# A filter moved into columns by transposes against a permutation, with the sign taken over by VectorE

## The chip, the cores and the metric

The kernel runs on one core of one Trainium2 chip. The metric is the device time of one execution in microseconds (us). All times below are us from the first instruction of the profiled execution unless they are marked ns. The engines are called as the profile calls them: PE is the matrix engine (PEld its weight loads), DVE is VectorE, ACT is ScalarE, POOL is GpSimd, SP is SyncE, whose queue issues most of the DMAs.

## The reference

A global filter in the frequency domain, followed by a mixture of experts in which each expert keeps at most 80 tokens:

```python
# x: (8, 2496, 256); filt_r, filt_i: (1249, 256), that is 2496 // 2 + 1 frequencies by 256 channels
X = np.fft.rfft(x, axis=1)
Y = X * (filt_r + 1j * filt_i)[None, :, :]
y = np.fft.irfft(Y, n=2496, axis=1)          # then reshaped to (19968, 256)

logits = y @ w_gate                          # w_gate: (256, 8)
expert_idx = np.argmax(logits, axis=1)       # gate_w: the softmax value of that expert
for e in range(8):                           # tokens of expert e, the 80 with the largest gate_w
    h = np.maximum(y[tok_idx] @ w1[e], 0.0)  # w1[e]: (256, 1024)
    out[tok_idx] = gate_w[tok_idx, None] * (h @ w2[e])
# all other rows of out are zero
```

## The kernel before

The transform of length 2496 is done as 39 by 64. The work has a first phase over "half batches" h (16 of them: 8 batches of 2 channel blocks of 128) and a second phase that picks tokens, rebuilds only the picked rows and runs the experts. The order of the instructions on every engine is written out by hand and kept; the framework only adds the semaphores. So a line further down in the program never overtakes a line above it on the same engine.

The first phase has 80 steps k, five for each half batch h. One step of the loop (from L969) writes, in this order:

- for k from 0 to 8 a filter turn (`next_filter`, L972; described below);
- `turn_t(k+1)` (L320): four PE transposes `pt` of 128x128 against the identity, then an ACT copy `t`;
- `stage2(k)` (L331): four matmuls `pb` against the table `d_t`;
- `filtered(k)` (L340): DVE multiplies the PSUM result by the filter `ft` into `p` (L346), and POOL adds and subtracts the halves into `yt` (L354, two instructions);
- from k = 4 on, one or two pieces of `stage1` of a later half batch (L304): matmuls `pa` against `wf_t` and an ACT copy `tt`;
- from k = 2 on `turn_y(k-2)` (L362): a DVE block transpose `u` of `yt`, whose result goes to DRAM (`yf`).

The filter arrives in rows and is needed in columns. `fst` is one tile of 128 partitions, 20 slots s and 256 channels. Partitions 0 to 63 hold the real part and 64 to 127 the imaginary part; in each half the lower 32 partitions are frequencies read upwards and the upper 32 are frequencies read downwards, so that those stand for the mirrored (conjugated) half of the spectrum. Partitions 96 to 127 are the mirrored imaginary rows. `filter_in(g)` (L497) issues four DMAs for a group g of four slots, two on SP's queue (real) and two on POOL's (imaginary), all five groups ahead of the loop. `filter_turn(g, cb)` (L506) multiplies the four slots of one channel block by a table `perm` of 0, 1 and -1, which orders the rows by frequency, and copies the result from PSUM to `ft`. There are ten turns: the first five are channel block 0 of g = 0 to 4, the last five are channel block 1. The first is written ahead of the loop with its copy on DVE (L910), the other nine stand at the top of the steps k = 0 to 8 with their copies on ACT, one step ahead of the `filtered` that needs them. Step k holds turn number k + 1.

The PSUM pool of these results has six buffers. `x` comes in three pieces for each batch through SP's queue; the pieces 3 to 6 are issued behind all of the real filter's DMAs, and the first `stage1` of the loop (step 4) reads the first of them.

Of the kernel before, what the change touches and what calls it, by code (L numbers as in the profile page):

```python
# [10 lines left out]
AL = mybir.AluOpType  # L11
# [19 lines left out]
SG, NG = 4, 5  # L31
# [15 lines left out]
def dft_tables():  # L47
    n1, n2 = np.arange(N1), np.arange(N2)
    s, q = np.arange(NS), np.arange(NQ)
    ph = 2 * np.pi * (np.outer(n1, s) % N1) / N1  # L50
    w = np.stack([np.cos(ph), -np.sin(ph)], 2)
    wf = np.zeros((N1, H3, NS, 2, H3))
    for h in range(H3):
        wf[:, h, :, :, h] = w

    slot = [J3 * h + j for j in range(20) for h in range(3)]
    slot += [J3 * h + j for j in range(20, J3) for h in range(2)]
    k = np.array([[next(m for m in range(i, S, N1) if m % NQ == j) for j in q] for i in s])
    th = 2 * np.pi * (n2[slot][:, None, None] * k % S) / S
    c, sn = np.cos(th), np.sin(th)  # L60
    d = np.zeros((2, N2, NS, 2, NQ))
    d[0, :, :, 0], d[1, :, :, 0] = c, sn
    d[0, :, :, 1], d[1, :, :, 1] = -sn, c

    two = np.where(s == 0, 1.0, 2.0) / S
    be = 2 * np.pi * (np.outer(q, n2) % NQ) / NQ
    back = np.zeros((2, NQ, 2, N2))
    back[0, :, 0], back[1, :, 0] = np.cos(be), -np.sin(be)
    back[0, :, 1], back[1, :, 1] = np.sin(be), np.cos(be)
    wi = np.zeros((4, SP, 2, N1, 4))  # L70
    for e in range(4):
        wi[e, :NS, 0, :, e] = (two * np.cos(ph)).T
        wi[e, :NS, 1, :, e] = (-two * np.sin(ph)).T

    n = (39 * n2[:, None] + 64 * n1) % S
    al = 2 * np.pi * (n.reshape(S, 1, 1) * k % S) / S
    rows = np.stack([np.cos(al), -np.sin(al)], 2) * two[:, None, None]
    at = np.arange(128)
    rows = rows.reshape(S, NS, 128)[:, :, 32 * (at % 4) + at // 4]
    rows = rows.reshape(S, NS, 4, 32).transpose(0, 2, 1, 3)  # L80

    perm = np.zeros((2, 2, 32, 2, NQ + NS - 1))
    for i in range(32):
        for up, t in enumerate((2 * 32 - 1 - i, i)):
            for j in range(NQ + NS - 1):
                if (j - 39 * t - NS + 1) % NQ == 0:
                    perm[0, 1 - up, i, 0, j] = 1.0
                    perm[1, 1 - up, i, 1, j] = 1.0 if up else -1.0
    f32 = np.float32
    return (wf.reshape(NP1, NM1).astype(f32), wi.reshape(4 * SP, 2, 4 * N1).astype(f32),  # L90
            d.reshape(128, NS, 128).astype(f32), back.reshape(128, 128).astype(f32),
            rows.reshape(S, NS * 128).astype(f32),
            perm.reshape(128, 2 * (NQ + NS - 1)).astype(f32))
# [3 lines left out]
def kernel(  # L97
# [11 lines left out]
    nc = tc.nc  # L109
    assert 1 <= cap <= 128  # L110
    cap1 = -(-cap * CAP1 // 80)

    wf_host, wi_host, d_host, e_host, rows_host, perm_host = dft_tables()
    wf_dram = nc.inline_tensor(wf_host, name="wf_tbl")
    wi_dram = nc.inline_tensor(wi_host, name="wi_tbl")
# [28 lines left out]
    def part_of(name, op, by, add=0.0):  # L144
# [26 lines left out]
                            op0=AL.mult, op1=AL.add)  # L171
    for b in range(B):
        nc.vector.tensor_scalar(out=cbase[:, b, :], in0=iota[:, 0:KC], scalar1=float(PB),
                                scalar2=4096.0 * b + 1.0, op0=AL.mult, op1=AL.add)
    nc.vector.tensor_scalar(out=cbase[:], in0=cbase[:], scalar1=trow[:, 0:1], scalar2=None,
                            op0=AL.add)
# [3 lines left out]
                            op0=AL.is_equal)  # L180
    thot = const([128, 16], F32, "thot")
    nc.vector.tensor_scalar(out=thot[:], in0=iota[:, 0:16], scalar1=trow[:, 0:1], scalar2=None,
                            op0=AL.is_equal)
    same_f = const([128, 128], F32, "same_f")
    with tc.tile_pool(name="setup", bufs=1) as su:
# [6 lines left out]
                                op0=AL.is_equal)  # L192
# [4 lines left out]
                            op0=AL.is_gt)  # L197
# [10 lines left out]
                            op0=AL.add)  # L208
# [45 lines left out]
    with tc.manual_schedule():  # L254
# [19 lines left out]
        perm = fwd.tile([128, 2, NQ + NS - 1], F32, name="perm")  # L274
        fst = late.tile([128, NS, C], F32, name="fst", tag="page0")
# [228 lines left out]
                                    ap=[[N1 * C, 32], [step, SG], [1, C]]))  # L504

        def filter_turn(g, cb, copy):  # L506
            ps = fps.tile([128, SG, 2, NQ], F32, name=f"pf_{g}_{cb}", tag="f")
            for i in range(SG):
                s = SG * g + i
                nc.tensor.matmul(out=ps[:, i], lhsT=fst[:, s, 128 * cb:128 * cb + 128],  # L510
                                 rhs=perm[:, :, NS - 1 - s:NS - 1 - s + NQ],
                                 start=True, stop=True)
            copy(out=ft[:, :, cb, SG * g:SG * g + SG, :].rearrange("p v s q -> p s v q"),
                 in_=ps[:])

# [298 lines left out]
        for i in range(5):  # L814
            nc.vector.tensor_scalar(out=shifted[:, i, :], in0=iota[:, 0:KR],
                                    scalar1=1.0 - (8 >> i), scalar2=None, op0=AL.add)
# [80 lines left out]
        def next_filter(copy):  # L897
            if turns:
                filter_turn(*turns.pop(0), copy)
# [69 lines left out]
        for k in range(NK):  # L969
# [8 lines left out]
            for h, i in s1_steps(k):  # L978
                stage1(h, i)
                hb, cb = divmod(h, NDB)  # L980
# [147 lines left out]
        for e in range(NH):  # L1128
            nc.gpsimd.indirect_dma_start(
                out=xg[e][:], out_offset=None, in_=y_sel[0:128 * (NR - 1), :],  # L1130
# [600 lines left out]
```

## Time and profile before

| what | value |
|---|---|
| runs | 407.19, 409.98 and 409.0 us (median 409.0) |
| the profiled execution, its own time | 407.02 us |
| its span, first to last instruction | 405.2 us |
| PE busy | 356.4 us, 88% of the span |
| DVE busy | 236.1 us, 58% |
| ACT busy | 132.8 us, 33% |
| POOL busy | 181.1 us, 45% |
| mean granted PE clock | 0.971 |

The profile has several views. The page gives the busy time of each engine, the chain of work that ended last (followed back from the last instruction, at each step to what released it) and the costliest groups of instructions: line, engine, operation, output <- inputs, count, then busy time and mean ns of one, then idle time ahead of them. The timeline merges neighbouring instructions of one line into a row: start, duration, engine, line, operation, names, shapes, count, and in brackets the engine's idle time ahead of the row and what ended it. PE records an ordinary float32 matmul as two passes, so a count of 8 can be four instructions (the ten filter turns are 40 matmuls and 80 records). The table by stretches gives for each stretch of time the busy time of each engine, the granted PE clock and the share of the DMA engines.

### The profile page before, as it was taken

How to read it: one execution, taken by the hardware profiler on the slowest of the kernel's cores; microseconds unless marked ns; L12 is line 12 of the kernel's file. 1: busy time of each engine (PE TensorE's matmuls, PEld its weight loads, DVE VectorE, ACT ScalarE, POOL GpSimd, SP SyncE). 2: the span in 40 equal slices, each digit the busy share in tenths (PEclk: the TensorE clock that was granted, in tenths of full speed). 3: DMA queues.
4: the chain of work that ended last, by engine and by line, in shares of the span. 5: the costliest groups of instructions: out<-in, count | busy, mean ns of one | idle time of the engine just before them, and what ended most of it. 6: DMA issues, size and time to landing. Idle time of an engine off the chain costs nothing.

```text
span 405.2 us, 9718 instructions
## 1 busy us (share of the span) xinstructions
PE 356.4 (88%) x3973; PEld 318.8 (79%) x3973; DVE 236.1 (58%) x485; ACT 132.8 (33%) x274; POOL 181.1 (45%) x248
## 2 busy tenths in 40 slices
PE   2879999999999999899999998979999857967970
PEld 2879979989989899699799896857875527957950
DVE  5025557766977858879798898299777400201100
ACT  1434545445445455354454452240100000101010
POOL 8335444644655545555457767730661010221220
PEclk9999999999999999999999999999999995989896
DMA  7998799999989989978999998999999995496000
GB/s 219 236 216 257 183 320 252 275 332 250 315 268 258 333 248 254 328 203 286 309 245 272 364 271 269 405 402 392 410 406 389 385 372 181 147 313 227 26 23 10
DMA packets 41099, 109.92 MB, mean 271 GB/s; under 512 B 4202, under 2 KB 14312, under 8 KB 39176
## 3 DMA queue, kind: packets, MB, share of 16 engines
q1 hardware_dynamic: 36534, 95.94, 74.0%
q0 software_dynamic: 4240, 13.15, 9.3%
q8 instruction: 33, 0.54, 0.5%
q10 hardware_dynamic: 274, 0.14, 0.1%
q14 instruction: 18, 0.15, 0.1%
HBM read 70.42 MB, written 40.37 MB: 273 GB/s over the span
## 4 chain that ended last, share of the span: by engine, by line
PE 49%; DMA 32%; issue 8%; POOL 3%; DVE 3%; ACT 2%; SPq 1%; POOLq 0%; ACTq 0%; DVEq 0%
PE pa L311 15%; PE pb L336 15%; PE pt L325 8%; DMA y_sel<-yr 7%; DMA x<-in_x_dram 6%; DMA out_dram<-ys_True,idxs 6%; DMA gt<-rows_tbl,idxr 4%; PE pz L390 4%; DMA page<-yf 3%; DMA xg_True<-y_sel,idxg 3%; PE pr L867 2%; DMA fst<-in_filt_r_dram 2%; ACT tt L316 1%; POOL gt L844 1%; PE py L402 1%
## 5 line engine op out<-in xcount | busy, mean ns | idle before, releaser
L354 POOL TENSOR_TENSOR yt<-p 128x256 f32<-128x256 f32 x156 | 113.5, 749 | 104.2 <-DVE p L346 95.5
L346 DVE TENSOR_TENSOR p<-pb,ft 128x1024 f32<-128x1024 f32 x80 | 97.2, 1217 | 53.1 <-PE pb L336 24.5
L311 PE MATMUL pa<-wf_t,x 117*128 117x120 f32 x704 | 92.7, 279 | 8.9 <-DMA x<-in_x_dram 8.2
L311 PEld LDWEIGHTS pa<-wf_t,x 117*128 117x128 f32 x704 | 86.9, 196 | 9.1 <-issue 7.6
L336 PE MATMUL pb<-d_t,t 128*128 128x128 f32 x640 | 84.6, 275 | 1.5 <-ACT t L329 1.5
L336 PEld LDWEIGHTS pb<-d_t,t 128*128 128x128 f32 x640 | 77.7, 192 | 1.9 <-ACT t L329 1.9
L316 ACT COPY tt<-pa 128x480 f32<-128x480 f32 x96 | 47.9, 516 | 91.3 <-PE pa L311 90.2
L867 PE MATMUL pr<-page,wt 128*32 128x256 f32 (+1 forms) x520 | 63.8, 380 | 1.8 <-DVE wt L855 1.0
L867 PEld LDWEIGHTS pr<-page,wt 128*32 128x32 f32 (+1 forms) x520 | 45.5, 134 | 16.2 <-issue 1.8
L325 PE MATMUL pt<-ident,tt 128*128 128x128 f32 x320 | 49.4, 276 | 3.7 <-ACT tt L316 3.7
L329 ACT COPY t<-pt 128x512 f32<-128x512 f32 x80 | 47.1, 589 | 16.1 <-PE pt L325 15.1
L367 DVE STREAM_TRANSPOSE u<-yt 128x512 f32<-128x512 f32 x70 | 49.0, 700 | 0.0
L844 POOL DMA_INDIRECT gt<-rows_tbl,idxr x28 | 29.7, 1060 | 31.6 <-DVE idxr L686 13.2
L325 PEld LDWEIGHTS pt<-ident,tt 128*128 128x128 f32 x320 | 36.5, 141 | 7.5 <-ACT tt L316 4.6
L855 DVE STREAM_TRANSPOSE wt<-gt 128x640 f32<-128x640 f32 x28 | 22.5, 828 | 13.8 <-DMA gt<-rows_tbl,idxr 13.0
L1221 POOL DMA_INDIRECT out_dram<-ys_True,idxs x8 | 7.5, 932 | 34.3 <-ACT ys_True L1219 21.7
L872 ACT COPY yr<-pr 128x256 f32<-128x256 f32 x7 | 2.7, 379 | 57.7 <-DMA y_sel<-yr 33.0
L1179 PE MATMUL ph_True<-xs_True,w 128*64 128x80 f32 x512 | 20.6, 244 | 0.0
L1179 PEld LDWEIGHTS ph_True<-xs_True,w 128*64 128x64 f32 x512 | 19.9, 147 | 0.1
L1197 PE MATMUL po_True<-hT_True,w 128*64 128x80 f32 x448 | 19.8, 255 | 0.0
L1197 PEld LDWEIGHTS po_True<-hT_True,w 128*64 128x64 f32 x448 | 18.7, 155 | 0.8 <-issue 0.4
L390 PE MATMUL pz<-yt,wg 128*32 128x512 f32 (+1 forms) x256 | 18.9, 435 | 0.0
(217 smaller groups left out, 282.1 us busy)
## 6 DMA issues: line engine op xcount, KB each, us to landing
out_dram<-zero_t SPq DMA_DIRECT2D x32, 624.0 KB
yf<-u SPq DMA_DIRECT2D x56, 320.0 KB
w<-in_moe_w_dram SPq DMA_DIRECT2D x16, 1024.0 KB
page<-yf SPq DMA_DIRECT2D x24, 640.0 KB
x<-in_x_dram SPq DMA_DIRECT2D x16, 936.0 KB
x<-in_x_dram SPq DMA_DIRECT2D x7, 702.0 KB
page<-yf POOLq DMA_DIRECT2D x4, 640.0 KB, 8.9
fst<-in_filt_r_dram SPq DMA_DIRECT2D x10, 128.0 KB
```

The costliest lines, as they stand in the source:

```text
L311: nc.tensor.matmul(out=ps[:, j, :], rhs=wf_t, start=True, stop=True, lhsT=xt[3 * b + ch][:, j0 + j - JC * ch, 128 * cb:128 * cb + 128])
L316: nc.scalar.copy(out=tt[h][:, :, H3 * j0:H3 * j0 + hn * jn].rearrange("p s (j h) -> p s j h", h=hn), in_=v)
L325: nc.tensor.transpose(ps[:, i, :], tt[h][:, 2 * s:2 * s + 2, :].rearrange("p r n -> p (r n)"), ident[:])
L329: nc.scalar.copy(out=t2[k][:], in_=ps[:])
L336: nc.tensor.matmul(out=ps[:, :, i, :], lhsT=t[:, i, :], rhs=d_t[:, SG * g + i, :], start=True, stop=True)
L346: nc.vector.tensor_tensor(out=p[:], in1=f.unsqueeze(2).to_broadcast(shape), op=AL.mult, in0=ps[:].rearrange("p r s q -> p r (s q)").unsque ...
L354: eng.tensor_tensor(out=y[:, :, 2 * r:2 * r + 2, :], in0=a, in1=b, op=op)
L367: nc.vector.transpose(uu[h][:, :, SG * g:SG * g + SG, :].rearrange("p a s w -> p s a w"), spectrum(h)[:, SG * g:SG * g + SG])
L390: nc.tensor.matmul(out=ps[32 * j:32 * j + 32].rearrange("p (s w) -> p s w", s=pn), lhsT=wg[:, cb, :], rhs=yt_t[:, (2 * b + cb) % 2, 5 * j ...
L867: nc.tensor.matmul(st["po"][c:c + w, :], lhsT=wts[r][:, s, c:c + w], rhs=yt_t[:, :, s] if b == B - 1 else columns(pages[b], s), start=(s = ...
L1179: nc.tensor.matmul(ph[c:c + 64, i, 0:cap], lhsT=w1[:, k, f:f + 64], rhs=xs[:, k, :], start=(k == 0), stop=(k == NDB - 1))
L1197: nc.tensor.matmul(po[c:c + 64, d, 0:cap], lhsT=w2[:, fc, 128 * d + c:128 * d + c + 64], rhs=hT[:, fc, :], start=(fc == 0), stop=(fc == NF ...
```

## The change

The host table `perm` loses its minus sign and so holds only zeros and ones, a plain permutation. The filter turn's matmuls are issued as transposes, with that permutation where the identity usually stands. The sign is put back by DVE: ahead of the first turn of each group (channel block 0), it multiplies partitions 96 to 127 of the group's four slots by -1 in place, 32 partitions of 1024 float32. That makes five new DVE instructions; the turns of channel block 1 read the same rows, negated already.

```diff
             for j in range(NQ + NS - 1):
                 if (j - 39 * t - NS + 1) % NQ == 0:
                     perm[0, 1 - up, i, 0, j] = 1.0
-                    perm[1, 1 - up, i, 1, j] = 1.0 if up else -1.0
+                    perm[1, 1 - up, i, 1, j] = 1.0
...
         def filter_turn(g, cb, copy):
+            if cb == 0:
+                low = fst[96:128, SG * g:SG * g + SG, :]
+                nc.vector.tensor_scalar(out=low, in0=low, scalar1=-1.0, scalar2=None,
+                                        op0=AL.mult)
             ps = fps.tile([128, SG, 2, NQ], F32, name=f"pf_{g}_{cb}", tag="f")
             for i in range(SG):
                 s = SG * g + i
                 nc.tensor.matmul(out=ps[:, i], lhsT=fst[:, s, 128 * cb:128 * cb + 128],
                                  rhs=perm[:, :, NS - 1 - s:NS - 1 - s + NQ],
-                                 start=True, stop=True)
+                                 is_transpose=True, start=True, stop=True)
             copy(out=ft[:, :, cb, SG * g:SG * g + SG, :].rearrange("p v s q -> p s v q"),
                  in_=ps[:])
```

The instructions of DVE in the first steps then stand in this order: negation 0, copy of turn 0, negation 1, `p` of step 0, negation 2, `p` of step 1, negation 3, `p` of step 2, `u`, negation 4, `p` of step 3.

## The prediction

> **What bounds the kernel now.** I read the page first, for the span and the chain that ended last.
>
> ```profile
> span 405.2 us, 9718 instructions
> PE 49%; DMA 32%; issue 8%; POOL 3%; DVE 3%; ACT 2%; SPq 1%; POOLq 0%; ACTq 0%; DVEq 0%
> ```
>
> PE is half of that chain and DMA a third, so the question is what the chain runs through where the filter turns stand. The chain in order of time, cut to the first 52 us and to the seam of the two phases, says it:
>
> ```profile
> 2.79 15.17 DMA x<-in_x_dram
> 17.98 8.86 DMA fst<-in_filt_r_dram
> 26.85 10.67 DMA x<-in_x_dram
> 37.66 1.12 PE pa L311 x8
> 38.79 0.90 PE pf L510 x8
> 39.69 0.44 PE pt L325 x4
> 40.12 0.89 PE pb L336 x8
> ...
> 241.35 1.12 SPq L829
> 242.52 6.79 DMA page<-yf
> ```
>
> The columns are start, duration and what. Up to 37.66 the end is set by arriving data: x, the filter, x again. From 37.66 PE follows PE, step by step, up to the seam near 241. A turn that ends at 37 or before is hidden by the x transfer; a turn behind 37.66 stands on the path. PE's timeline places the turns (`pf`):
>
> ```profile
> 21.95 1.06 PE L510 MATMUL pf<-perm,fst 128*128 128x128 f32 x8
> 24.19 1.13 PE L510 MATMUL pf<-perm,fst 128*128 128x128 f32 x8 [1.18 <-DMA fst<-in_filt_r_dram]
> 25.60 1.06 PE L336 MATMUL pb<-d_t,t 128*128 128x128 f32 x8
> 26.97 1.13 PE L510 MATMUL pf<-perm,fst 128*128 128x128 f32 x8 [0.32 <-DMA fst<-in_filt_r_dram]
> 30.05 1.13 PE L510 MATMUL pf<-perm,fst 128*128 128x128 f32 x8 [0.62 <-DMA fst<-in_filt_r_dram]
> 32.44 1.13 PE L510 MATMUL pf<-perm,fst 128*128 128x128 f32 x8
> 34.73 1.06 PE L510 MATMUL pf<-perm,fst 128*128 128x128 f32 x8
> 37.66 1.12 PE L311 MATMUL pa<-wf_t,x 117*128 117x120 f32 x8 [0.54 <-DMA x<-in_x_dram]
> 50.20 1.50 PE L311 MATMUL pa<-wf_t,x 117*128 117x120 f32 x12
> ```
>
> Turns 0 to 5 start at 21.95 to 34.73, ahead of the x wait; turns 6 to 9 (steps 5 to 8) lie between 37.66 and 50.20. The x wait itself is only 0.54 us: anything that lengthens the steps before it by more than that moves the path.
>
> **The change part by part.** *What it removes.* A turn is four matmuls, and the page's transposes are the nearest row for their new form:
>
> ```profile
> L510 PE MATMUL pf<-perm,fst x80: 273/273/348, 21.9 to 48.8; 128*128 128x128 f32 x80
> L325 PE MATMUL pt<-ident,tt 128*128 128x128 f32 x320 | 49.4, 276 | 3.7 <-ACT tt L316 3.7
> ```
>
> Ten turns of four matmuls are 80 records, two passes each; 80 groups of four transposes are 320, one pass each. In the chain eight passes of a turn take 0.90 us and four of `pt` 0.44, so a turn gets 0.45 us shorter. All ten would give 4.5 us; the four behind 37.66 give 4 x 0.45 = 1.8 us on the path, and the six before it nothing, as long as the x wait covers them. That the rows of `perm` are not the identity should not alter the pass count; if it does, see the rivals.
>
> *What it adds.* Five DVE instructions of 32 x 1024 float32, and each of the first five turns now waits for one. No row shows this form. The nearest:
>
> ```profile
> L815 DVE TENSOR_SCALAR shifted<-iota 128x16 f32<-128x16 f32 x5 | 0.6, 163 | 0.0
> L187 DVE TENSOR_SCALAR m_i<-iota_i 128x128 int32<-128x128 int32 x1 | 0.2, 219 | 0.0
> L191 DVE TENSOR_SCALAR same_f<-m_f,lane 128x128 f32<-128x128 f32 x1 | 0.3, 278 | 0.0
> ```
>
> Constant operand: 163 ns at 16 elements, 219 at 128, so 0.5 ns an element and 219 + 896 x 0.5 = 667 ns at 1024. With a per-partition operand: 278 at 128, which against 163 is 1.03 ns an element and 278 + 896 x 1.03 = 1.2 us. The negation has a constant operand; I take 0.67 us, and 1.2 as the upper end.
>
> Its data do not hold it up. The imaginary rows come through POOL's queue:
>
> ```profile
> 4.47 4.54 POOL L501 DMA_DIRECT2D fst<-in_filt_i_dram  x8
> 13.94 0.55 POOL L501 DMA_DIRECT2D fst<-in_filt_i_dram  x1 [0.83 <-DMA fst<-in_filt_i_dram]
> DMA to landing us min/median/max: 7.9/8.6/11.6
> ```
>
> Groups 0 to 3 are issued by 9.0 and so landed by 20.6 at the longest, group 4 by 26.1. No DMA is moved, and SP's and POOL's queues are passed by nothing new.
>
> *Where the wait falls.* DVE executes in the written order, and negation g stands behind `p` of step g - 2:
>
> ```profile
> 23.05 0.69 DVE L513 COPY ft<-pf 128x512 f32<-128x512 f32 x1 [15.81 <-PE pf L510]
> 26.69 1.23 DVE L346 TENSOR_TENSOR p<-pb,ft 128x1024 f32<-128x1024 f32 x1 [2.95 <-PE pb L336]
> 33.85 0.70 DVE L367 STREAM_TRANSPOSE u<-yt 128x512 f32<-128x512 f32 x1
> ```
>
> So a ring closes that was open before: `p` (DVE), negation (DVE), next turn (PE), `pt`, `pb` (PE), `p` again. Before, PE ran ahead of DVE and the turn waited at most for its DMA. While PE waits at a turn, the transposes, `pb` and, from step 4, `pa` wait behind it, and ACT's copies behind those. The ring from rows: a hop between engines 0.04 (the copy at 23.05 starts 0.04 behind 21.95 + 1.06); turn to `pb` start 25.60 - 24.19 = 1.41, less 0.45, 0.97; `pb` start to `p` start 26.69 - 25.60 = 1.09; `p` 1.23; negation 0.67. One round is 4.00 us.
>
> - Negation 0 is done long before 21.95. Turn 0 ends 0.45 earlier, its copy is done at 23.30, negation 1 at 23.97: turn 1 still starts at 24.19, when its real rows arrive. No loss.
> - Turn 1 at 24.19, `pb` 25.16, `p` 26.25 to 27.48, negation 2 to 28.15, turn 2 at 28.19 (before: 26.97).
> - One round on: turn 3 at 32.19 (before: 30.05). Its data came at 30.05, so the ring decides.
> - `p` of step 2 ends at 35.48. Behind it now stands `u`, 0.70 with 0.08 overlapped: 36.10. Negation 4 to 36.77, turn 4 at 36.81 (before: 32.44).
> - Turn 5 needs no negation, the ring ends. `pb` of step 3 at 37.78, then eight passes (0.89), turn 5 and `pt` (0.45 each), `pb` of step 4 (0.89): the first `pa` at 40.45. The x wait is over by then and gone; what was late last, x, is replaced by the ring.
>
> That is 40.45 - 37.66 = 2.8 us late. Turns 6 to 9 give 1.8 back: **1.0 us late** at the row 50.20.
>
> *Contention.* POOL starts its two additions right behind `p`, and DVE and POOL can block each other:
>
> ```profile
> 28.00 1.41 POOL L354 TENSOR_TENSOR yt<-p 128x256 f32<-128x256 f32 x2 [5.29 <-DVE p L346]
> 113.38 0.14 DVE L467 TENSOR_SCALAR gw<-gw 128x39 f32<-128x39 f32 x1
> 161.83 1.41 POOL L354 TENSOR_TENSOR yt<-p 128x256 f32<-128x256 f32 x2 [1.20 <-DVE p L346]
> 162.69 0.59 DVE L467 TENSOR_SCALAR gw<-gw 128x39 f32<-128x39 f32 x1
> ```
>
> The same small constant-operand instruction takes 0.14 us at 113.38 and 0.59 at 162.69, ending at 163.28 where POOL's pair ends (163.24). The Trainium skill, page "SBUF — State Buffer", section "SBUF: two separate sides", calls it an exclusive lock held for a whole instruction by whichever of the two came first; by that rule, with which 162.69 agrees, a negation that comes second waits and one that comes first makes POOL wait. POOL starts 0.08 behind the end of `p` (28.00 against 27.92). Negations 2 and 3 are next on DVE and need no signal, so I let them win: cost nothing, `yt` some 0.6 later, which nothing in these steps waits for (`u` of it is two steps on). Negation 4 comes 0.62 behind the end of `p`, inside POOL's pair, which lasts to 0.08 + 1.41 = 1.49: it waits 0.17 (to the pair's middle, 0.79) to 0.87 us. I take 0.2, as one instruction ended the wait at 162.69.
>
> *Sum.* -1.8 + 2.8 + 0.2 = +1.2 us. From 50 to 241 the chain names engines alone and no DMA, and the loads at the seam are issued by those steps in order, so I carry it to the end one for one. The profiled execution took 407.02, which is 405.2 and 1.8 around it, and would take 408.2. The median of the runs shown is 409.0, which becomes **410.2 us**, 0.3% up.
>
> **The rivals.**
>
> *A. The ring is cheaper than drawn, faster.* If the negations left PE's order as it is (ring hidden whole behind the x transfer), only the 1.8 us would stay: 407.2. For it: DVE is idle between its rows there (2.95 ahead of 26.69). Against it: the queue's order, and an x slack of 0.54.
>
> *B. Dearer negations.* At 1.2 us each, negation 1 ends at 24.50 and delays turn 1 by 0.35, and three rounds grow by 0.53: +1.9 more, 412.1. If POOL wins the lock each time, negations 2 and 3 wait one or two instructions, 0.7 to 1.4 each, and negation 4 up to 0.7 more: 411.6 to 413.7. The first has against it that L191 has an operand of another kind; the second, POOL's start 0.08 behind.
>
> *C. The clock drops, slower.* PE would now idle from the end of `pb` to the next turn: 25.16 + 0.89 to 28.19 is 2.1 us, twice, and once 2.9. The tail shows what a gap can do:
>
> ```profile
> 367.59 2.44 PE L1197 MATMUL po_True<-hT_True,w 128*64 128x80 f32 x64
> 374.88 0.53 PE L1164 MATMUL px_True<-ident,xg_True 80*128 80x80 f32 x2 [2.29 <-DMA xg_True<-y_sel,idxg]
> 375.33 3.66 PE L1197 MATMUL po_True<-hT_True,w 128*64 128x80 f32 x64
> 265.00:266.20 1.20, 0.00 (x0) 0.00 (x0) 1.17 (x4) 1.20 (x4) 0.90 (x2) 1.00 1.04 410
> ```
>
> A gap of 2.29 was followed by 64 passes in 3.66 instead of 2.44; yet the stretch at 265 lies in a longer gap and its granted clock (third number from the end) is 1.00. One drop costs about 1.2: 411.4. If the clock halves and stays so for the three rounds, 16 passes of 0.11 double in each, 1.8 a round, 5.3 in all: 415.5. It is slower by over 1% (4.1 us) from the second such round on: 1.2 + 2 x 1.8 = 4.8. The Trainium skill, page "TensorE: Matmul & The Clock Gate", section "Part 4: PE-mode transpose", says that transposes do not count as activity to the clock gate; by that rule the new turns and `pt` would be idle time to it and only `pb` would hold the clock, which gives the long form, 415.5. No row of before shows such a mix with gaps of that length.
>
> *D. The permutation runs at two passes.* Nothing saved: four turns behind 37.66 and five in or behind the ring keep their 0.45, +4.0: 414.2. It would show as 80 records again.
>
> **How the numbers follow.** The forecast has 0.58, A 0.10, B 0.15, C 0.12 (two thirds of it the single drop), D 0.03, and 0.02 is for the order of the last DMAs falling otherwise. The runs of one kernel lie 2.8 us apart (407.19 to 409.98), so one per cent, 4.1 us, is about what tells a change from none. The forecast alone spans 409.4 to 411.5. The range takes in A and most of B and the single drop, with that scatter at the ends: 406.8 to 413.5. Faster by over 1% (below 404.9) lies under every case, 0.04. Slower by over 1% (above 413.1) takes C's long form, D and the top of B, 0.11. The rest, 0.85, is no change.
>
> **What would show it.** 40 `pf` records in place of 80, a turn of 0.45 us. Five DVE rows on `fst` of about 0.67 us, the last with a wait. PE waiting for DVE at turns 2, 3 and 4, 2.1 + 2.1 + 3.1 = 7.3 us in all. No wait for x ahead of the first `pa` of the loop, which starts at 40.5 to 40.8. Later steps moved by 1.0 to 1.4. Wrong if the negations run ahead of `p`, if the clock reads under 1.00 between 26 and 41, or if the seam or the tail gives back or adds more than the shift.

## The result, and the profile after

| | before | after |
|---|---|---|
| median of the runs | 408.25 us (405.13 to 412.43) | 413.11 us (410.14 to 417.15) |
| profiled execution, its own time | 407.02 | 415.02 |
| its span | 405.2 | 413.2 |
| its mean granted PE clock | 0.971 | 0.955 |

The ratio of after to before is 1.0135 [1.0109, 1.016]: slower by 1.35%, about 5.5 us, where 1.2 us was forecast. Carried to the median of 409.0 that the forecast started from, it gives 414.5, past the upper end of the range (413.5) and in the class to which 0.11 was given. The ratios here leave out executions in a slower state that some runs fall into, and are not the quotient of the two medians, which would be 1.0119.

From the page of the changed kernel: the span, the granted clock of PE in 40 slices (10.3 us each, tenths of full speed), and the chain by engine.

```profile
span 413.2 us, 9641 instructions
PEclk9986899999999999999999999989999997989995
PE 63%; DMA 13%; issue 10%; DVE 6%; ACT 3%; another core or an unknown queue 2%; POOL 1%; POOLq 0%; ACTq 0%; DVEq 0%
```

Before, DMA held 32% of the chain; now 13%, and PE 63%. Most of that difference lies behind the seam of the two phases: in the opening the chain held 34.7 us of transfers before and holds 23.2 now. The x transfer no longer sets the end of the opening. The new thing is in the clock: the third to fifth slices, 20.7 to 51.7 us, read 8, 6, 8. The timeline of PE on the changed kernel shows what lies there (start, duration, form, count, idle time ahead and what ended it):

```profile
24.08 0.93 PE L514 MATMUL pf<-perm,fst 128*128 128x128 f32 x4 [1.82 <-DMA fst<-in_filt_r_dram]
25.66 1.91 PE L336 MATMUL pb<-d_t,t 128*128 128x128 f32 x8
29.65 0.63 PE L514 MATMUL pf<-perm,fst 128*128 128x128 f32 x4 [2.08 <-issue]
30.56 1.06 PE L336 MATMUL pb<-d_t,t 128*128 128x128 f32 x8
33.77 0.63 PE L514 MATMUL pf<-perm,fst 128*128 128x128 f32 x4 [2.16 <-issue]
34.83 1.92 PE L336 MATMUL pb<-d_t,t 128*128 128x128 f32 x8
39.64 1.09 PE L514 MATMUL pf<-perm,fst 128*128 128x128 f32 x4 [2.89 <-issue]
41.37 1.92 PE L336 MATMUL pb<-d_t,t 128*128 128x128 f32 x8
45.66 1.05 PE L311 MATMUL pa<-wf_t,x 117*128 117x120 f32 x8
56.28 1.50 PE L311 MATMUL pa<-wf_t,x 117*128 117x120 f32 x12
```

Turns 1 to 4 stand at 24.08, 29.65, 33.77 and 39.64. PE sits idle 2.08, 2.16 and 2.89 us ahead of the last three, as drawn. But the same eight passes of `pb` take 1.06 us in one round and 1.91 in the others. The first `pa` of the loop follows at 45.66 without any wait for x, and the row that stood at 50.20 stands at 56.28: 6.08 later. The table by stretches, changed kernel first, then the kernel before (the third number from the end is the granted clock):

```profile
24.00:26.00 2.00, 1.92 (x10) 1.95 (x11) 0.00 (x0) 0.69 (x2) 0.00 (x0) 0.56 1.03 252
30.00:32.00 2.00, 1.62 (x15) 1.42 (x13) 0.28 (x1) 1.08 (x2) 0.82 (x2) 1.00 0.89 234
32.00:34.00 2.00, 0.23 (x2) 0.26 (x3) 1.64 (x2) 0.00 (x0) 0.97 (x1) 1.00 0.85 278
36.00:38.00 2.00, 0.75 (x4) 0.45 (x3) 1.04 (x1) 0.00 (x0) 0.00 (x0) 0.50 0.83 258
40.00:42.00 2.00, 2.00 (x11) 2.00 (x10) 0.00 (x0) 0.92 (x2) 0.12 (x1) 0.50 0.85 246
22.00:48.00 26.00, 17.05 (x105) 16.15 (x104) 11.45 (x13) 7.19 (x14) 8.45 (x11) 0.74 0.79 214
```

```profile
22.00:48.00 26.00, 23.34 (x202) 22.60 (x202) 12.89 (x14) 10.76 (x21) 10.60 (x16) 1.00 0.82 220
```

Over the same 26 us PE had 1.00 before and 0.74 after, with two stretches at half clock (from 24 to 28 and from 34 to 45). Next the operations of the change, from the views by tile (`pf` and `fst`), and the rows of DVE and POOL in the ring:

```profile
L514 PE MATMUL pf<-perm,fst x40: 270/271/446, 21.7 to 54.8; 128*128 128x128 f32 x40
L509 DVE TENSOR_SCALAR fst<-fst x5: 690/691/707, 13.8 to 38.8; 32x1024 f32<-32x1024 f32 x5
```

```profile
27.61 1.23 DVE L346 TENSOR_TENSOR p<-pb,ft 128x1024 f32<-128x1024 f32 x1 [3.90 <-PE pb L336]
28.86 0.69 DVE L509 TENSOR_SCALAR fst<-fst 32x1024 f32<-32x1024 f32 x1
38.10 0.70 DVE L367 STREAM_TRANSPOSE u<-yt 128x512 f32<-128x512 f32 x1
38.83 0.71 DVE L509 TENSOR_SCALAR fst<-fst 32x1024 f32<-32x1024 f32 x1
```

```profile
28.92 1.91 POOL L354 TENSOR_TENSOR yt<-p 128x256 f32<-128x256 f32 x2 [6.23 <-DVE p L346]
38.26 1.86 POOL L354 TENSOR_TENSOR yt<-p 128x256 f32<-128x256 f32 x2 [3.32 <-DVE p L346]
```

There are 40 records in place of 80: the permutation runs in one pass. The five negations take 0.69 us each. Negation 2 starts 0.02 behind `p`, ends at 29.55, and turn 2 starts at 29.65. POOL's pair beside it takes 1.91 instead of 1.41: POOL, not DVE, paid for running side by side.

### The profile page after: what moved, and what is told of

The parts are those of the page before. It is cut to its first block, busy times and chain, and to the rows that moved or that the text cites. A ratio compares the mean times of both kernels' runs of the same rounds, so it can differ in the third digit from the quotient of the medians.

```text
span 413.2 us, 9641 instructions
## 1 busy us (share of the span) xinstructions
PE 358.2 (87%) x3933; PEld 318.7 (77%) x3933; DVE 239.7 (58%) x490; ACT 133.1 (32%) x274; POOL 182.0 (44%) x248
## 4 chain that ended last, share of the span: by engine, by line
PE 63%; DMA 13%; issue 10%; DVE 6%; ACT 3%; another core or an unknown queue 2%; POOL 1%; POOLq 0%; ACTq 0%; DVEq 0%
PE pb L336 17%; PE pa L311 15%; PE pr L871 11%; PE pt L325 9%; DMA out_dram<-ys_True,idxs 5%; PE pz L390 4%; DMA fst<-in_filt_r_dram 4%; DMA x<-in_x_dram 2%; PE pf L514 1%; DMA xg_True<-y_sel,idxg 1%; ACT tt L316 1%; PE py L402 1%; PE pv L413 1%; DVE p L346 1%
## 5 line engine op out<-in xcount | busy, mean ns | idle before, releaser
L354 POOL TENSOR_TENSOR yt<-p 128x256 f32<-128x256 f32 x156 | 114.8, 757 | 108.9 <-DVE p L346 100.2
L336 PE MATMUL pb<-d_t,t 128*128 128x128 f32 x640 | 87.1, 281 | 1.5 <-ACT t L329 1.5
L336 PEld LDWEIGHTS pb<-d_t,t 128*128 128x128 f32 x640 | 80.3, 197 | 1.9 <-ACT t L329 1.9
L871 PE MATMUL pr<-page,wt 128*32 128x256 f32 (+1 forms) x520 | 65.7, 383 | 2.3 <-issue 1.3
L871 PEld LDWEIGHTS pr<-page,wt 128*32 128x32 f32 (+1 forms) x520 | 47.0, 137 | 17.1 <-issue 3.8
L325 PE MATMUL pt<-ident,tt 128*128 128x128 f32 x320 | 50.9, 283 | 3.7 <-ACT tt L316 3.7
L325 PEld LDWEIGHTS pt<-ident,tt 128*128 128x128 f32 x320 | 37.7, 145 | 7.5 <-ACT tt L316 4.6
```

What stands on the lines that cost most here:

```text
L325: nc.tensor.transpose(ps[:, i, :], tt[h][:, 2 * s:2 * s + 2, :].rearrange("p r n -> p (r n)"), ident[:])
L336: nc.tensor.matmul(out=ps[:, :, i, :], lhsT=t[:, i, :], rhs=d_t[:, SG * g + i, :], start=True, stop=True)
L354: eng.tensor_tensor(out=y[:, :, 2 * r:2 * r + 2, :], in0=a, in1=b, op=op)
L871: nc.tensor.matmul(st["po"][c:c + w, :], lhsT=wts[r][:, s, c:c + w], rhs=yt_t[:, :, s] if b == B - 1 else columns(pages[b], s), start=(s = ...
```

## The experiments

Two theories stood against each other for the 5.5 us. **Clock:** the ring costs what was forecast, and its gaps cost the rest through PE's clock. **Ring:** the ring alone, through dearer rounds, lock or queue, costs it all. The texts put on record ahead of the runs number three: their theory 1 is the clock theory (the ring makes gaps, the gaps let the clock halve), theory 2 says that the clock falls because transposes do not count as activity of PE, whatever the negations do, and theory 3 that the loss is made in the second phase. Each kernel is compared with the kernel before on the same chip; `pf`, `pa` and `pb` are the names used above.

**1. The same wait, with the gaps filled.** The changed kernel, with PE given plain matmuls of the identity into an unused PSUM tile ahead of turns 1 to 4, so many that they end just before the negation does.

```diff
             ps = fps.tile([128, SG, 2, NQ], F32, name=f"pf_{g}_{cb}", tag="f")
+            if cb == 0 and g:
+                for _ in range((0, 6, 8, 8, 11)[g]):
+                    nc.tensor.matmul(out=st["hold"][:, 0:128], lhsT=ident[:], rhs=ident[:],
+                                     start=True, stop=True)
```

> The changed kernel with its ring left as it is, but PE is kept busy in the gaps: 6, 8, 8 and 11 plain matmuls of the identity by itself, into a PSUM tile that nobody reads, stand ahead of turns 1 to 4 (12, 16, 16 and 22 passes of 0.11 us). Theory 1: the granted clock stays at 1.00 from 24 to 46, turns 2, 3, 4 start near 28.2, 32.2 and 36.9, the first pa at 40.5 to 40.8, and what remains is the ring's 1.0 to 1.4 us: ratio 1.003. If the clock is not what the rest of the loss comes from, the ratio stays at 1.013 with the clock at 1.00.

Measured: 406.89 us, ratio 1.0029 [0.9998, 1.0059]. PE's timeline and the table by stretches of this kernel:

```profile
27.07 1.95 PE L513 MATMUL hold<-ident 128*128 128x128 f32 x16
29.31 0.63 PE L518 MATMUL pf<-perm,fst 128*128 128x128 f32 x4 [0.30 <-issue]
35.22 2.62 PE L513 MATMUL hold<-ident 128*128 128x128 f32 x22
38.27 0.63 PE L518 MATMUL pf<-perm,fst 128*128 128x128 f32 x4 [0.44 <-issue]
22.00:48.00 26.00, 24.57 (x217) 23.92 (x216) 13.70 (x16) 9.67 (x19) 11.97 (x16) 1.00 0.82 222
```

The turns come no earlier than the negations let them: 25.27, 29.31, 33.43, 38.27, rounds of 4.04, 4.12 and 4.84, and the first `pa` at 41.84. (This execution began about a microsecond later, its turn 0 at 23.00.) From turn 1 to the first `pa` are 16.57 us; in the changed kernel they are 45.66 - 24.08 = 21.58. Useless work on PE, the order untouched, takes 5.0 us out of that stretch and most of the loss out of the time. That shows the clock theory; the ring theory would have left the ratio at 1.0135.

**2. The filling done by transposes.** The same with twice as many transposes, which take one pass each.

```diff
-                for _ in range((0, 6, 8, 8, 11)[g]):
-                    nc.tensor.matmul(out=st["hold"][:, 0:128], lhsT=ident[:], rhs=ident[:],
-                                     start=True, stop=True)
+                for _ in range((0, 12, 16, 16, 22)[g]):
+                    nc.tensor.matmul(out=st["hold"][:, 0:128], lhsT=ident[:], rhs=ident[:],
+                                     is_transpose=True, start=True, stop=True)
```

> As the run that held PE busy with plain matmuls in the ring's gaps, but the filling is done by transposes: 12, 16, 16 and 22 of them, one pass of 0.11 us each, so the same busy time. If the clock follows PE's activity of either kind: clock 1.00 from 24 to 46, ratio 1.003 again. If transposes do not count for the gate: the clock reads 0.5 in stretches as in the changed kernel though PE is never idle for more than 0.5 us, and the ratio is 1.010 to 1.02.

Measured: 408.99 us, ratio 1.0031 [1.0, 1.0062]. From its PE timeline and its table by stretches:

```profile
25.99 1.91 PE L513 MATMUL hold<-ident 128*128 128x128 f32 x16
28.24 0.63 PE L518 MATMUL pf<-perm,fst 128*128 128x128 f32 x4 [0.34 <-issue]
22.00:48.00 26.00, 24.27 (x216) 23.43 (x215) 14.78 (x17) 9.61 (x20) 11.03 (x15) 1.00 0.80 216
34.41:37.82 3.41, 2.92 (x28) 2.71 (x26) 2.56 (x3) 0.00 (x0) 1.87 (x2) 1.00 0.84 250
```

The clock stays at 1.00 and the ratio is that of the plain filling. The stretch from 34.41 to 37.82 holds no plain matmul at all, only 2.92 us of transposes, and the clock is 1.00 in it and behind it. So float32 transposes hold the clock here as plain matmuls do. The rule of the Trainium skill that stood behind rival C ("TensorE: Matmul & The Clock Gate", "Part 4: PE-mode transpose": transposes don't count as activity) isn't borne out by this run; the gaps themselves let the clock fall.

**3. The negation alone, with plain matmuls.** `is_transpose=True` is taken out; sign and order stay as in the changed kernel.

```diff
-                                 is_transpose=True, start=True, stop=True)
+                                 start=True, stop=True)
```

> Half of the change: the negations where the change put them and the permutation without its sign, but plain matmuls of two passes instead of transposes. Theory 1: the ring has rounds of 4.4 to 4.5 us, turn 4 starts at about 38, the first pa at about 43, 5.3 us late with nothing given back, and the clock halves in the gaps of about 2 us as in the changed kernel: ratio 1.013 to 1.025. Theory 2: the same ring, but the clock stays at 1.00, since no turn is a transpose: ratio 1.013.

Measured: 415.36 us, ratio 1.0222 [1.0164, 1.028]. PE's timeline and a stretch:

```profile
33.76 1.13 PE L514 MATMUL pf<-perm,fst 128*128 128x128 f32 x8 [2.15 <-issue]
40.00:42.00 2.00, 2.00 (x11) 2.00 (x11) 0.00 (x0) 0.59 (x1) 0.00 (x0) 0.50 0.88 266
```

The gaps are the same (2.08, 2.15, 2.89) and the rounds 0.5 longer (4.54 against 4.04 in experiment 8, 4.61 against 4.12). The clock falls to 0.50 here as well, with no transposed turns, though in this execution only behind the last gap. The turns' being transposes is not the cause of the loss.

**4. The turns alone, without the negation.** The five DVE instructions are dropped; the sign of the mirrored imaginary rows is left out.

```diff
-            if cb == 0:
-                low = fst[96:128, SG * g:SG * g + SG, :]
-                nc.vector.tensor_scalar(out=low, in0=low, scalar1=-1.0, scalar2=None,
-                                        op0=AL.mult)
```

> The other half: transposes against the unsigned permutation and no negation at all; it leaves out the sign of the mirrored imaginary rows. Theory 1: as with the negations ahead, no ring, first pa at about 37.7, ratio 0.996. Theory 2: the clock falls between 24 and 46 and the ratio is above 1.005.

Measured: 404.86 us, ratio 0.9959 [0.9922, 0.9997], which is 1.7 us less (the interval reaches from 0.1 to 3.2); 1.8 us is what four turns at 0.45 were to bring. The first `pa` waits for x again (0.83) and starts at 37.03. The whole loss of the change hangs on the negations.

**5. Short negations in the same place.** The same instruction over 4 of 256 channels; the sign of the other channels is left out.

```diff
-                low = fst[96:128, SG * g:SG * g + SG, :]
+                low = fst[96:128, SG * g:SG * g + SG, 0:4]
```

> The changed kernel with its five negations where they stand, but each only over 4 of the 256 channels (32 x 16 elements instead of 32 x 1024); it leaves out the sign of the other channels. If the order on DVE makes the wait: a negation takes about 0.16 us, a round of the ring 3.5 us, turns 2, 3 and 4 at 27.7, 31.2 and 35.3, still waiting for DVE with gaps of 1.6, 1.6 and 2.4 us; with the clock at 1.00 the first pa at about 38.9 and the ratio 0.999, with one or two drops of the clock 1.003 to 1.01. If the negations' length makes it: no wait, first pa at 37.7, ratio 0.996.

Measured: 408.66 us, ratio 1.0025 [0.9991, 1.0059]. PE's timeline:

```profile
27.89 0.63 PE L514 MATMUL pf<-perm,fst 128*128 128x128 f32 x4 [1.57 <-DVE fst L509]
31.49 0.63 PE L514 MATMUL pf<-perm,fst 128*128 128x128 f32 x4 [1.64 <-DVE fst L509]
```

A negation of 0.17 us still makes PE wait 1.57 and 1.64 us, for `p` that stands ahead of it; the rounds are 3.52 and 3.60, shorter by the 0.52 that the negation lost. The wait comes from the place in DVE's order. The first `pa` came at 39.38, and in this execution the clock did not fall, though one gap was 2.37. The ratio's interval takes in both forecasts, the one with drops of the clock and the one without, so the rows and not the time decide here.

**6. The negations ahead.** Negations 0 to 3 are written ahead of turn 0, negation 4 behind turn 0's copy, all ahead of the first `p`.

```diff
+        def negate(g):
+            low = fst[96:128, SG * g:SG * g + SG, :]
+            nc.vector.tensor_scalar(out=low, in0=low, scalar1=-1.0, scalar2=None,
+                                    op0=AL.mult)
...
-            if cb == 0:
-                low = fst[96:128, SG * g:SG * g + SG, :]
-                nc.vector.tensor_scalar(out=low, in0=low, scalar1=-1.0, scalar2=None,
-                                        op0=AL.mult)
...
+        for g in range(4):
+            negate(g)
         next_filter(nc.vector.tensor_copy)
+        negate(4)
```

> The changed kernel, but the negations of groups 0 to 3 stand ahead of the first turn on DVE and that of group 4 right behind turn 0's copy, so none stands behind a p. Theory 1 (the ring through DVE makes PE idle, and the idle gaps let the clock halve): no turn waits for DVE, the first pa of the loop starts at the x arrival, about 37.7, the turns behind it give back 1.8 us, granted clock 1.00 from 38 on; about 406.5 against 408.25, ratio 0.996. Theory 2 (transposes do not count for the clock gate, so the clock falls with them whatever the negations do): the clock reads 0.5 for some stretches between 24 and 46 here too, and the ratio stays above 1.005. Theory 3 (the loss is made in the second phase, by transfers that fall otherwise): the first phase gains and the ratio stays near 1.01.

Measured: 404.73 us, ratio 0.9985 [0.9953, 1.0017]. Rows of DVE, POOL and PE:

```profile
20.81 2.92 DVE L508 TENSOR_SCALAR fst<-fst 32x1024 f32<-32x1024 f32 x1 [0.75 <-DMA fst<-in_filt_i_dram]
20.82 2.36 POOL L839 MEMSET gt<- 128x640 f32 x4
37.66 1.12 PE L311 MATMUL pa<-wf_t,x 117*128 117x120 f32 x8 [1.32 <-DMA x<-in_x_dram]
```

The ring is open again: the first `pa` waits for x, the clock is 1.00 in every stretch from 22 to 48, and the row that was at 50.20 stands at 48.36. The loss is gone. So theory 2 falls, since the turns are still transposes, and theory 3, since the ratio isn't near 1.01. A gain isn't shown: 0.996 was expected, and the interval holds both it and 1. One negation took 2.92 us beside POOL's four memsets and held up turn 0's copy and so turn 1 (24.57).

**7. One negation later.** As in 6, with only negations 0 to 2 ahead (`range(3)`) and 3 and 4 behind the copy, clear of the memsets.

> The changed kernel with the negations of groups 0 to 2 ahead of the first turn and those of groups 3 and 4 behind turn 0's copy on DVE, past POOL's four memsets. No negation is held for over 1 us, turn 1 starts at its data, the first pa at the x arrival, 37.7, and from there as with the negations ahead: 1.8 us gained, ratio 0.996, since turn 1's delay was hidden behind x in that run too.

Measured: 408.17 us, ratio 0.9976 [0.9935, 1.0018]. PE's timeline and a stretch:

```profile
38.69 1.12 PE L311 MATMUL pa<-wf_t,x 117*128 117x120 f32 x8 [3.15 <-DMA x<-in_x_dram]
40.00:42.00 2.00, 2.00 (x13) 2.00 (x12) 0.00 (x0) 1.48 (x3) 0.00 (x0) 0.56 0.89 275
```

Turn 1 is early (23.88), and no negation was held (0.69 each). But x came late in this execution, a microsecond behind what was expected, PE, now faster, waited 3.15 us for it, and the clock fell behind that wait. So the saved time can turn into a gap and be paid for in clock. The interval doesn't tell this kernel from 6, from the kernel before or from the 0.996 that was expected.

**8. The changed kernel, profiled again.** No edit.

> The changed kernel once more, for a second look at its first 60 us. The ring's rounds are 4.0 to 4.1 us wherever the clock reads 1.00, and 1 to 2 us longer wherever it reads 0.5; the drops need not fall in the same gaps as in the first look. The first pa lies between 40.5 (no drop) and 46.

Measured: 412.85 us, span 411.1. From its PE timeline and its table by stretches:

```profile
27.93 0.63 PE L514 MATMUL pf<-perm,fst 128*128 128x128 f32 x4 [2.09 <-DVE fst L509]
32.95 1.08 PE L514 MATMUL pf<-perm,fst 128*128 128x128 f32 x4 [2.15 <-issue]
30.00:32.00 2.00, 0.79 (x4) 0.50 (x3) 1.10 (x1) 0.00 (x0) 0.00 (x0) 0.50 0.88 225
```

Here the round from turn 1 (23.89) to turn 2 is the one at full clock, 4.04 us, and those behind it take 5.02 and 6.53; the clock is 0.50 from 30 to 42, where the first profile had 1.00 from 28 to 34. The first `pa` is at 44.46. The drop is in both profiles, at other gaps.

**9. Ahead, and with fillers.** As in 7, with plain matmuls of the identity: 5, 2 and 3 ahead of turns 1 to 3, and 5 ahead of the loop's first `stage1`.

```diff
+        def hold(n):
+            for _ in range(n):
+                nc.tensor.matmul(out=spare[:, 0:128], lhsT=ident[:], rhs=ident[:],
+                                 start=True, stop=True)
...
             if cb == 0:
+                hold((0, 5, 2, 3, 0)[g])
...
+            if k == 4:
+                hold(5)
```

> The kernel with the negations ahead (groups 0 to 2 before turn 0, 3 and 4 behind its copy), and PE kept busy in the waits for data that are left: 5, 2 and 3 plain matmuls of the identity ahead of turns 1, 2 and 3, and 5 ahead of the first pa, where PE waits for x. If the clock is what ate the rest of the gain there, it now reads 1.00 from 22 to 48 in each run and the ratio is 0.995 to 0.996 (1.8 us). If the gain is lost elsewhere, the ratio stays near 0.998.

Measured: 404.33 us, ratio 0.9948 [0.9914, 0.9983], the fastest version with the whole computation, and clear of both kernels. Its first `pa` in PE's timeline:

```profile
38.30 1.12 PE L311 MATMUL pa<-wf_t,x 117*128 117x120 f32 x8 [1.09 <-DMA x<-in_x_dram]
```

The clock is 1.00 from 22 to 48, and the row of 50.20 is at 49.00. That the fillers make it better than 6 or 7 isn't shown: the intervals overlap.

**10. The kernel before, profiled again.** No edit.

> The kernel before once more, for a second look: the clock at 1.00 from 20 to 50, the turns waiting for data alone, the first pa at the x arrival within 1 us of 37.7.

Measured: 408.75 us, span 407.0. The clock is 1.00 from 22 to 48, the longest gap ahead of a turn 1.42; the first `pa` waits 1.55 for x and starts at 39.18, later than expected. The arrival of x moves by over a microsecond between executions, so a shift of that size at 37.66 can't be read from one profile.

## Why the prediction was wrong

**The step that failed** is the sum's silent one: each round was priced at the clock of before, 1.00, and the clock stood apart as rival C with 0.12, two thirds of it a single drop of 1.2 us. The working had the gaps right (2.1, 2.1 and 2.9 us) and had a row of the tail in which a gap of 2.29 was followed by a slow stretch; it weighed that against a stretch near 265 at 1.00 and let the latter carry. But a granted clock in a stretch where PE does nothing says little of what the next burst will get: in the changed kernel the stretch from 32 to 34, with PE busy for 0.23 us, also reads 1.00, and the `pb` behind it, at 34.83, runs at half speed. The term is 21.58 - 16.57 = 5.0 us in the profiled executions, and in the timed runs the difference of the ratios 1.0135 and 1.0029, 1.06% or 4.3 us, give or take some 1.6 by the two intervals. That is near the 5.3 of C's long form and far from its single drop (1.2), but the 5.3 was right in part by luck: it doubled three rounds, while one round ran at full clock and 2.45 of the 5.0 us came behind the ring, from turn 4 to the first `pa` (6.02 us against 3.57 in experiment 1).

Point by point, by the steps of the sum:

- *The ring.* Forecast 4.00 a round; 4.12 (turn 2 to 3, at full clock) and 4.04 (experiments 1 and 8). The third round, with `u` in it, was drawn at 4.62 and takes 4.84 in experiment 1. The waits of PE ahead of turns 2 to 4 were to add up to 7.3 us and are 7.13. The wait for x is gone, as said.
- *The negation.* 0.67 forecast, 0.69 measured. Rival B's 1.2 us falls.
- *The lock.* Negations 2 and 3 win, as assumed, and POOL pays 0.5 us a pair. Negation 4 was to wait 0.2 and did not: it starts 0.03 behind `u`, 0.57 behind the start of POOL's pair, and takes 0.71, and POOL's pair grew to 1.86 instead. So this row does not bear out that whoever comes second waits, as far as POOL's spans, which are rough, can tell. The 0.2 was over-priced, and the longer rounds happened to make up for it: from turn 1 to the first `pa` are 16.57 in experiment 1, where 40.45 - 24.19 + 0.2 = 16.46 were forecast.
- *The turn.* 0.45 shorter, as forecast, and rival D falls (40 records). From the first `pa` to the row behind turn 9 were 50.20 - 37.66 = 12.54 and are 56.28 - 45.66 = 10.62: 1.92 back, with 1.8 forecast. Experiment 4 has the gain by itself, 1.7 us.
- *The sum without the clock.* Forecast +1.2 us (0.3%); with the clock held, 1.0029 and 1.0031, each interval from about 0 to 2.5 us. The mechanism stands by the rows, and the times agree with its size.
- *Rival A* falls: the negations do not run ahead of `p` unless they are written there.

The clock fell through gaps, not through transposes; experiments 2 and 3 show both halves of that. *When it falls.* The length of one gap doesn't say it. Gaps of 2.08 to 2.16 were followed now by full, now by half clock in the same kernel, a gap of 1.82 was followed by half, and one of 2.37 by none. The Trainium skill, "TensorE: Matmul & The Clock Gate", "Part 1: The HAM clock gate (the "warmup" mystery)", says that activity is judged in free-running windows of 3413 ns, so that the point of a change varies from run to run. The traces agree: in all twelve profiles each stretch of half clock that ends within the trace, and each of full clock between two of them, lasts a multiple of 3.41 us (at half clock 3.41 and 10.24 in the changed kernel, 13.65 in experiment 8), and the grid lies otherwise in each execution. The table by stretches of the changed kernel, cut on that grid (PE's busy time is the number behind the length):

```profile
20.84:24.26 3.42, 1.60 (x15) 1.39 (x15) 1.38 (x2) 1.02 (x3) 1.85 (x4) 1.00 0.99 215
24.26:27.67 3.41, 3.31 (x16) 3.01 (x14) 0.06 (x1) 1.17 (x2) 0.00 (x0) 0.50 1.00 226
27.67:31.08 3.41, 1.43 (x13) 1.46 (x14) 1.85 (x2) 0.76 (x2) 1.91 (x2) 1.00 0.93 217
31.08:34.50 3.42, 1.26 (x12) 1.10 (x12) 1.92 (x2) 0.39 (x2) 1.47 (x2) 1.00 0.83 263
34.50:37.91 3.41, 2.25 (x12) 1.95 (x9) 0.95 (x1) 1.11 (x2) 0.44 (x1) 0.50 0.84 238
37.91:41.32 3.41, 1.68 (x8) 1.71 (x9) 1.59 (x3) 0.56 (x1) 1.86 (x2) 0.50 0.81 221
41.32:44.74 3.42, 3.42 (x18) 3.42 (x17) 1.25 (x2) 1.18 (x3) 0.00 (x0) 0.50 0.83 261
```

The windows with 1.60 and 1.26 us of work are followed by half clock, the one with 1.43 is not, and the clock comes back behind the windows with 3.31 and 3.42. Counted over the twelve traces, 57 of the 62 windows at full clock in which PE was busy for less than half the time were followed by half clock, and none of the 1224 busier ones. So it is PE's share of a window that tells: a round of the ring at full clock has 1.95 us of work in 4.04, 48%, while the rounds of experiments 3 (2.46 in 4.54) and 5 (1.96 in 3.52) lie above half, and there the clock fell only behind the longest gap or not at all. This is counted after the fact, no run was made to test it, and why 5 windows passed stays open. The same page's rule in "Why this matters for your kernels", no idle gaps over some 3 us, would have let these gaps pass; the measured 0.50 behind gaps of 1.8 to 2.9 decides against reading it as a safe limit.

**What stays open** is the tail: the profiled span grew by 8.0 where the row at 56.28 had moved 6.08; the timed runs give 5.5. Up to the seam the shift stays (`pr`, at 247.76 before, is at 253.85). Then copies of ACT wait for what the profile calls another core or an unknown queue, the `pk` of 266.26 stands at 276.01, and a part is made up later. Such waits stand in the profiles of experiments 2, 5, 7 and 8 too, and not in that of 1; since 1 and 2 have the same ratio, they are not what makes the loss. Their cause is not known.

## What to carry to other kernels

A cheap instruction written behind a consumer of PE's output, on an engine that works in order, ties PE's next step to that consumer: price the whole ring, not the instruction, and write it ahead where its data allow. Then price each new gap on PE twice, once for its length and once for the work behind it at half clock; gaps of 2 us in rounds of 4 were enough for that here, and what told was the share of time that PE worked. A few useless matmuls in the gap tell the two prices apart: in experiment 1 they held the clock and left the order as it was.

## What the runs showed of the hardware that was not expected

- PE's clock changed on a grid of 3.41 us, and fell to half behind windows in which PE was busy for less than half the time (57 of 62 of them, and none of 1224 busier ones), so idle times of 1.8 to 3.2 us were enough. In a ring of rounds of 4 us with 2 us of work it stayed there for up to 13.65 us (28.8 to 42.4 in experiment 8). Where in the ring it falls varies between executions.
- Transposes in float32 take one pass of about 0.11 us, with a permutation as with the identity, and they held the clock (1.00 in experiment 2, through a window of transposes alone).
- A negation of 0.69 us took 2.92 when it started 0.01 us ahead of POOL's four memsets (experiment 6), and 0.69 when it stood behind them (experiment 7): the wait was not bounded by one instruction of the other side.
